# Order of work in the first four units of a fused linear attention and feed-forward kernel

## Chip, cores and metric

One core of one Trainium2 chip. The metric is the device time of one execution in microseconds (us), the median of the runs. The engines are called PE (matrix products), DVE (vector), ACT (scalar), POOL (GpSimd) and SP (the queue that issues nearly all transfers).

## What is computed

A gated linear attention is computed per batch and head, and its output goes through a feed-forward block with the "quick" GELU:

```python
# q, k, v, f_logit: (4, 8, 768, 48) float32
f = 1 / (1 + exp(-f_logit))
for t in range(768):
    state = f[:, :, t, :, None] * state + k[:, :, t, :, None] * v[:, :, t, None, :]
    y[:, :, t] = q[:, :, t] @ state
x = y.transpose(0, 2, 1, 3).reshape(3072, 384)
h = x @ w_in                      # w_in: (384, 2048), float64 in memory
g = h / (1 + exp(-1.702 * h))
out = g @ w_out                   # w_out: (2048, 384), float64 in memory
```

## The kernel before

**Units.** The 3072 tokens are cut into 12 units of 256 (three per batch), called `n` = 0 to 11 in the code and one to twelve in the titles of changes; here "unit one" is `n` = 0. `attention(n)` builds the pieces of one unit: for 64-token chunks the scores between tokens are built in six levels (distances 1, 2, 4 to 32). At each level PE multiplies queries by a copy of the keys (`score`, tile `sc`, line 416), DVE multiplies queries and keys by the decays of the next level (`promote`, L510 in the first units, L514 later), ACT copies the keys, and from unit four on the queries too, aside for the next level (`set_aside`, `Kc` L485 and `Qc` L491), and the scores are put through a mask into the matrix A (`evacuate`: level 0 by a multiplication on DVE, L457; the middle levels by predicated copies on DVE, L476; the last by four copies on ACT, L466). Then PE multiplies A by v into `y` (`add`, L525), PE forms each chunk's key-value sums (L634, into `pd` or the banks of `sc`), DVE rolls the states `st` forward (L655 to L659), PE adds the states' part to `y` (L680), ACT copies `y` to `yT` in eight pieces (L692), and transfers make `xT` of it (L723, L728), the input of the feed-forward block.

**Turning the inputs.** `turn` brings f, q and k into the layout with the head's channels on partitions: by PE transposes and ACT copies (L354, L359) for units one to three, by DVE transposes (L342) from unit four on. `half_up` (POOL, L369) finishes the decay's sigmoid, and `begin_gates` (POOL, L407) multiplies decays over growing distances into `tot`. `reverse_v` is DVE's shuffle of v (L306). `begin_f`, `begin`, `begin_k` and `begin_gates` start the next unit.

**Weights.** w_in and w_out arrive as 64-bit floats in 16 pieces. Each is converted by one ACT operation (L225, begun by `begin_pair`) and four DVE operations (L227 to L230). `convert` does one DVE operation at a time and asks for the next transfer after each piece. `merge(n, ..., pieces)` spreads `pieces` times two of these operations over unit `n`.

**Order.** PE's and POOL's order is the program's throughout. For units one to four (`opening`, then `merge` with `n` = 1, 2, 3) the order of all engines is written by hand up to `fill_order.close()`; after that a scheduler orders DVE, ACT and SP. `merge` walks the parts of a unit (`parts_of`) and puts feed-forward products of earlier units (`h` L1070, `o` L1084) between them as filling. In `parts_of` the last part of a unit, `inter` (the states' part of `y`, `yT` and `xT`), is run at the head of the next unit's first part, by `both`, for every `n` from 1 on. In unit three (`merge` with `n` = 2) the next unit, `n` = 3 = `N_FILL`, is begun by `begin_k`, which turns k, sets `Kc` and `Qc` aside and promotes.

**Banks.** The tile `sc` and the tile `y` have one buffer each of two PSUM banks; four further banks (`bank`) are handed round. `level(l)`, for units two and three, takes `sc` for every level:

```python
        def level(l):
            scores()
            score(0, l, queries(l))
            promote(l)
            evacuate(l)
            if l == 2:
                reverse_v(n)
```

Of the kernel before, what the change touches and what calls it, by code (L numbers as in the profile page):

```python
# [16 lines left out]
def view(t, offset, dims):  # L17

    a = t[:]
    return bass.AP(a.tensor, a.offset + offset, [list(a.ap[0])] + [list(d) for d in dims])  # L20
# [3 lines left out]
def kernel(  # L24
# [34 lines left out]
    B, H, S, D = q.shape  # L59
    DM = H * D  # L60
# [11 lines left out]
    NL = len(LEV)  # L72
# [4 lines left out]
    N_FILL = 3  # L77
# [49 lines left out]
    R = U // 32  # L127
# [64 lines left out]
    state = {"fetch": 0, "begin": 0, "done": 0, "behind": 0}  # L192
# [111 lines left out]
    def reverse_v(n):  # L304

        nc.vector.stream_shuffle(vts[n][:, 0], vrs[n], list(range(31, -1, -1)))  # L306
# [9 lines left out]
    def attention(n):  # L316
# [11 lines left out]
        parts = []  # L328
# [4 lines left out]
        def slot(s):  # L333
            return X[:, s]

        def turn(j, outs, fn=None, pieces=None):

            if n >= N_FILL:
                for f in (1, 0):
                    out = outs(f)  # L340
                    at, step = (0, 1) if f else (HALF - 1, -1)
                    nc.vector.transpose(  # L342
                        view(out, at, [[HALF, NP], [step, R4], [R4 * step, 32]]),
                        by_half[:, j, f].rearrange("p a (j d) -> p (a j) d", j=R4)[:, :, :32],
                    )
                if fn:
                    fn()
                return
            for j0 in pieces or range(0, R, 4):
                pt = bank([P, 4, P], f"t_{n}_{j}_{j0}")  # L350
                for jj in range(4):
                    for h in range(2):
                        x = (j0 + jj) * D
                        nc.tensor.matmul(  # L354
                            pt[h * HS:(h + 1) * HS, jj, :], lhsT=by_pair[j][:, h, x:x + HS], rhs=ident, start=True, stop=True
                        )
                for f in (1, 0):
                    at, step = (j0, 1) if f else (HALF - 1 - j0, -1)
                    nc.scalar.activation(  # L359
                        view(outs(f), at, [[HALF, NP], [R * step, 16], [step, 4]]),  # L360
                        pt.rearrange("p j (a f i) -> p f a i j", a=NP, f=2)[:, 1 - f],
                        (AF.Tanh if n else AF.Sigmoid) if fn else AF.Copy, scale=0.5 if fn and n else 1.0,
                    )
            if fn and n and (not pieces or R - 4 in pieces):
                half_up()


        def half_up():
            nc.gpsimd.tensor_scalar(F, F, 0.5, 0.5, op0=ALU.mult, op1=ALU.add)  # L369
# [18 lines left out]
            if n >= N_FILL or (n == 1 and 1 == 0):  # L388
                load_raw(n + 1, 1)

        def begin_k():
            turn(2, lambda f: slot((KR, KF)[f]))
            if n >= N_FILL or (n == 1 and 2 == 0):
                load_raw(n + 1, 2)
            if n >= N_FILL:
                set_aside(0, True)
                promote(0)
            else:
                set_aside(0)
# [35 lines left out]
        def scores(tag="sc"):  # L435
            new = ps.tile([P, 2, NP, 2, HS], F32, tag=tag, name=f"sc_{n}_{next(serial)}")
            t["sc"], t["both"] = (new[:, 0], new[:, 1]), [(0, new.rearrange("p h a s t -> p (h a) s t"))]
            return new
# [41 lines left out]
        def set_aside(l, q_too=False):  # L480


            m = LEV[l]
            c = t["Kc", l] = att.tile([P, SLOT], F32, tag="Kc", name=f"Kc_{n}_{l}", bufs=2)
            nc.scalar.copy(  # L485
                c.rearrange("p (n two m) -> p n two m", two=2, m=m),
                view(X, KF * SLOT, [[2 * m, SLOT // (2 * m)], [(KR - KF) * SLOT + m, 2], [1, m]]),
            )
            if q_too:
                c = t["Qc", l] = att.tile([P, 2, SLOT // 2], F32, tag="Qc", name=f"Qc_{n}_{l}", bufs=2)  # L490
                copied["aside"] = nc.scalar.copy(  # L491
                    c.rearrange("p f (n m) -> p f n m", m=m),
                    view(X, QR * SLOT, [[(QF - QR) * SLOT + m, 2], [2 * m, SLOT // (2 * m)], [1, m]]),
                )
# [35 lines left out]
                        )  # L530

        def level(l):
            scores()
            score(0, l, queries(l))
            promote(l)
            evacuate(l)
            if l == 2:
                reverse_v(n)
# [180 lines left out]
        def to_x(y, x, ng, hs=range(2)):  # L719

            for h in hs:
# [3 lines left out]
                while at < D:  # L725
# [4 lines left out]
                    )  # L730
                    at += w

        return (begin_f, begin, begin_k, begin_gates), parts, (open_level, open_evacuate, turn_k), lambda: reverse_v(n)

# [408 lines left out]


    units = [attention(n) for n in range(NALL)]
    LAG = 18 * DM

    def parts_of(n):  # L1150

        parts = list(units[n][1])
        _, inter = parts.pop()
        if n:
            kind, scores = parts[0]
            _, ahead = units[n - 1][1][-1]
            def both():
                rest = ahead()
                scores()
                if rest:  # L1160
                    rest()
            parts[0] = kind, both
        if n + 1 < NALL:
            begin_f, begin, begin_k, begin_gates = units[n + 1][0]
            i = len(parts)
            if n + 1 < N_FILL:

                parts.append(("K", lambda: (begin_k(), begin_gates())))
                kind, head = parts[0]
                parts[0] = kind, lambda: (head(), load_raw(n + 1, 1), keep_up(1))  # L1170
                parts.insert(4, ("B", lambda: (begin(), load_raw(n + 1, 2))))
                parts.insert(2, ("B", begin_f))
            else:
                kind, states = parts.pop()
                if n in CARRY:
                    parts += [("B", begin_f), ("B2", begin), ("S1", lambda: (states(), begin_gates())), ("K3", begin_k)]
                elif n < N_FILL:
                    second = parts[1][1]
                    parts[1] = parts[1][0], lambda: (second(), [load_raw(n + 1, j) for j in range(3)])
                    parts += [("B", begin), (kind, lambda: (states(), begin_gates())), ("B", begin_k)]  # L1180
                    parts.insert(i - 3, ("B", begin_f))
                else:
                    parts += [("B", begin_k), (kind, lambda: (states(), begin_gates()))]
                    parts.insert(i - 3, ("B", lambda: (begin_f(), begin())))
        else:
            parts.append(("W", inter))
        return parts
# [49 lines left out]
    UNIT = NFF * NK * U + U // P * NFF * DM  # L1237
    H20 = 20 * FG * G

    def opening():  # L1240

        begin_f, begin, begin_k, begin_gates = units[0][0]
        next_f, next_q, next_k, next_gates = units[1][0]
        level, evacuate, turn_k = units[0][2]
        load_raw(0, 0)
        load_raw(0, 2)
        load_raw(0, 1, (nc.scalar,))
        fetch_weights()
        begin_f()
        begin_gates()  # L1250
        begin_k()
        begin()
        load_raw(1, 0)
        load_raw(1, 2)
        load_v(0)
        load_raw(1, 1)
        fetch_weights()
        fetch_weights()
        for l in range(NL):
            chosen[:] = [2, 3][l % 2:][:1]  # L1260
            level(l)
            if l in (2, 3):
                next_f((0, 4)[l - 2:][:1])
            elif l < NL - 1:
                keep_up(1)
            if l == 1:
                begin_pair(0)
                state["begin"] = 1

        nc.scalar.activation(q_end, q_end, AF.Gelu_apprx_sigmoid)  # L1270
        chosen[:] = [2, 3]
        turn_k(0)
        turn_k(2)
        evacuate(0)
        evacuate(NL - 1)
        for l in range(1, NL - 1):
            evacuate(l)
            if l == 2:
                units[0][3]()
        chosen[:] = [2, 3, 2, 3]  # L1280
        next_q()
        units[0][1][-2][1]()
        next_gates()
        for _ in range(NOP):
            convert()

    fill = []
# [1 line left out]
    fill += mlp_blocks((0, 0)) + mlp_blocks((0, 1))  # L1289
    merge(1, fill, UNIT // 2 - LAG // 2 - 3 * DM, steady, 13, hold=1)  # L1290
    fill += mlp_blocks((1, 0), (1, 1)) + mlp_blocks((0, 2), (1, 2))
    merge(2, fill, UNIT + 3 * DM, steady, 10)
    fill += mlp_blocks((2, 0), (2, 1)) + mlp_blocks((2, 2), (0, 3)) + mlp_blocks((1, 3), (2, 3))
    w_sums = [*sums_of_w(("c3", "p15", "c2", "p6"))]
    merge(3, fill, 3 * UNIT // 2 - LAG // 2, steady, 7, by=0.7, chores=w_sums, per=1)
    fill_order.close()
    for n in range(N_FILL, NALL):
        fill += mlp_unit(n, fill)
# [42 lines left out]
```

## Time and profile before

| | |
|---|---|
| median of 3 runs | 611.32 us (608.47, 611.32, 612.24) |
| the profiled execution | 609.87 us, its span 608.0 us |
| mean granted clock of PE | 0.986 |
| PE busy | 579.3 us, 95% of the span |
| DVE, ACT, POOL busy | 436.0 (72%), 291.4 (48%), 139.2 (23%) us |
| transfers | 58.29 MB, mean 96 GB/s |

The span runs from the first to the last instruction. "Busy" counts an engine's instructions that compute; the granted clock is the share of full speed at which PE was let run. The page's 40 slices (15.2 us each; digits are busy tenths) show where PE is not full:

```profile
PE   7869899969999999999999999999999999999897
DVE  2797976565894867788867888868778686462284
PEclk9979999979999999999999999999999999999999
```

The opening and unit two fill the first five slices or so; unit three ends in the ninth (122 to 137 us). From 140 us on PE idles little. Instructions are listed with the line of the kernel, the engine, the operation and out<-in; an fp32 product of PE stands in the records twice.

### The profile page before, as it was taken

Reading aid. Unit: us, or ns where it says so; the run is one execution under the profiler, and the core shown is the slowest. Engines: PE = TensorE matmul, PEld = TensorE weight load, DVE = VectorE, ACT = ScalarE, POOL = GpSimd, SP = SyncE. Lnnn points to the kernel's source line nnn. Section 1 sums busy time; section 2 is a strip of 40 time slices with the busy share of each in tenths; the row PEclk is TensorE's granted clock in tenths of the full one; section 3 lists DMA queues with packets and bytes.
Section 4 is the critical chain, followed back from the end, with each engine's and each line's share of the span. In section 5 each row is a group of like instructions: output and inputs, shape, how many; then the busy total and the mean of one; then the engine's idle time right before and its main releaser. Section 6 shows DMA issues by size and latency. Waiting matters only on the chain.

```text
span 608.0 us, 18479 instructions
## 1 busy us (share of the span) xinstructions
PE 579.3 (95%) x7814; PEld 517.4 (85%) x7814; DVE 436.0 (72%) x696; ACT 291.4 (48%) x613; POOL 139.2 (23%) x215
## 2 busy tenths in 40 slices
PE   7869899969999999999999999999999999999897
PEld 6656676847677689999999999999999999999897
DVE  2797976565894867788867888868778686462284
ACT  4655643433332444456465474575474563552440
POOL 3030110050032523240421312502502502303000
PEclk9979999979999999999999999999999999999999
DMA  7856866652034245245443253443362111001000
GB/s 190 195 139 150 191 150 176 149 135 71 1 95 101 78 125 131 49 115 132 92 127 90 60 133 98 119 124 70 89 154 55 57 53 29 27 3 26 27 1 26
DMA packets 83314, 58.29 MB, mean 96 GB/s; under 512 B 33633, under 2 KB 75265, under 8 KB 83233
## 3 DMA queue, kind: packets, MB, share of 16 engines
q1 hardware_dynamic: 82896, 56.73, 37.5%
q8 instruction: 61, 1.00, 0.7%
q10 hardware_dynamic: 337, 0.39, 0.3%
q14 instruction: 20, 0.16, 0.1%
HBM read 43.98 MB, written 8.39 MB: 86 GB/s over the span
## 4 chain that ended last, share of the span: by engine, by line
PE 71%; DVE 12%; ACT 6%; DMA 4%; issue 3%; POOL 2%; SPq 2%; DVEq 0%; ACTq 0%; POOLq 0%
PE h L976 14%; PE h L1070 10%; PE o_Y L839 9%; PE o L1084 8%; PE o_Z L839 6%; PE sc L416 6%; PE h_y L976 5%; PE o_X L839 3%; PE o_W L839 3%; PE t L354 2%; ACT yT L692 2%; POOL tot L407 2%; PE y L680 1%; DVE g L1004 1%; DVE X L342 1%
## 5 line engine op out<-in xcount | busy, mean ns | idle before, releaser
L1070 PE MATMUL h<-xT,w_in 128*128 128x256 f32 x384 | 89.0, 387 | 1.6 <-DMA xT<-yT 1.6
L485 ACT COPY Kc<-X 128x512 f32<-128x512 f32 x72 | 48.2, 670 | 78.4 <-DVE X L514 57.4
L1070 PEld LDWEIGHTS h<-xT,w_in 128*128 128x128 f32 x384 | 73.1, 193 | 13.3 <-DMA xT<-yT 1.8
L514 DVE TENSOR_TENSOR X<-X,tot 128x1024 f32<-128x1024 f32 x45 | 57.4, 1275 | 35.7 <-PE sc L416 26.4
L1084 PE MATMUL o<-w_out,g 128*128 128x384 f32 x192 | 67.3, 500 | 3.7 <-DVE w_out L230 3.3
L1084 PEld LDWEIGHTS o<-w_out,g 128*128 128x128 f32 x192 | 36.1, 194 | 27.0 <-DVE w_out L230 4.1
L407 POOL TENSOR_TENSOR tot<-F 128x512 f32<-128x512 f32 x12 | 12.5, 1039 | 198.0 <-DVE st L658 192.3
L976 PE MATMUL h<-E,w_in 128*128 128x128 f32 (+1 forms) x420 | 53.4, 275 | 0.0
L839 PE MATMUL o_Y<-T,S 128*128 128x192 f32 x288 | 50.6, 329 | 0.0
L976 PEld LDWEIGHTS h<-E,w_in 128*128 128x128 f32 x420 | 50.1, 192 | 0.0
L1074 ACT ACTIVATE g<-h 128x256 f32<-128x256 f32 x64 | 24.0, 383 | 54.4 <-PE h L1070 54.1
L1006 ACT ACTIVATE g<-g 128x512 f32<-128x512 f32 (+1 forms) x63 | 35.5, 582 | 25.8 <-DVE g L1004 25.4
L839 PEld LDWEIGHTS o_Y<-T,S 128*128 128x128 f32 x288 | 46.8, 190 | 0.5
L692 ACT COPY yT<-y 48x256 f32<-48x256 f32 x96 | 35.1, 366 | 22.3 <-PE y L680 21.1
L476 DVE COPY_PREDICATED A<-masks,sc 128x256 f32<-128x256 uint32 (+1 forms) x98 | 42.1, 503 | 1.7 <-ACT A L466 1.6
L369 POOL TENSOR_SCALAR F<-F 128x1024 f32<-128x1024 f32 x11 | 16.1, 1461 | 111.5 <-ACT F L372 91.5
L1004 DVE TENSOR_TENSOR g<-g,h 128x512 f32<-128x512 f32 (+1 forms) x52 | 31.7, 631 | 12.5 <-PE h L976 11.5
L342 DVE STREAM_TRANSPOSE X<-raw 128x512 f32<-128x512 f32 x36 | 38.1, 1107 | 0.2
L416 PEld LDWEIGHTS sc<-X,Kc 48*64 48x64 f32 x1440 | 26.6, 138 | 12.1 <-ACT Kc L485 6.6
L416 PE MATMUL sc<-X,Kc 48*64 48x64 f32 x1440 | 31.2, 224 | 5.6 <-ACT Kc L485 2.7
L938 POOL TENSOR_TENSOR E<-xT 128x128 f32<-128x128 f32 (+1 forms) x32 | 17.7, 562 | 74.4 <-DMA xT<-yT 33.0
L1004 DVE TENSOR_TENSOR g<-g,h_y 128x512 f32<-128x512 f32 (+1 forms) x26 | 16.5, 633 | 22.0 <-PE h_y L976 21.1
(159 smaller groups left out, 1180.9 us busy)
## 6 DMA issues: line engine op xcount, KB each, us to landing
bits<-in_moe_w_out_dram SPq DMA_DIRECT2D x8, 768.0 KB
raw<-in_f_logit_dram SPq DMA_DIRECT2D x48, 96.0 KB
raw<-in_k_dram SPq DMA_DIRECT2D x48, 96.0 KB
bits<-in_moe_w_in_dram SPq DMA_DIRECT2D x8, 576.0 KB
raw<-in_q_dram SPq DMA_DIRECT2D x44, 96.0 KB
k_tok<-z SPq DMA_DIRECT2D x56, 64.0 KB
kt<-k_tok SPq DMA_DIRECT2D x14, 256.0 KB
xT<-yT SPq DMA_DIRECT2D x24, 144.0 KB
```

The source lines that it names most:

```text
L342: nc.vector.transpose(view(out, at, [[HALF, NP], [step, R4], [R4 * step, 32]]), by_half[:, j, f].rearrange("p a (j d) -> p (a j) d", j=R4) ...
L416: nc.tensor.matmul(t["sc"][h][g * HS:(g + 1) * HS, a, s, :], lhsT=t["Kc", l][rows(h), x:x + HS], rhs=rhs(h, a, g), start=True, stop=True,)
L476: moved = nc.vector.copy_predicated(out=view(A, c * HALF + at, dims), mask=mask.bitcast(U32), data=got)
L485: nc.scalar.copy(c.rearrange("p (n two m) -> p n two m", two=2, m=m), view(X, KF * SLOT, [[2 * m, SLOT // (2 * m)], [(KR - KF) * SLOT + m, ...
L514: nc.vector.tensor_tensor(x, x, y, ALU.mult)
L692: nc.scalar.copy(view(yT[rows(h)], at, [[U, NP], [step, HS]]), py[columns(h, g), g, :, f, :])
L839: nc.tensor.matmul(t[name], lhsT=lhs(f), rhs=rhs(f), start=(new and i == 0), stop=(i == HF - 1), skip_group_check=True,)
L976: nc.tensor.matmul(ph[:, t], lhsT=WA[a][:, f * P:(f + 1) * P], rhs=E[n][b], start=(root and t == 0), stop=not goes_on, skip_group_check=True,)
L1004: nc.vector.tensor_tensor(to, to, part, ALU.add if sign > 0 else ALU.subtract)
L1006: nc.scalar.activation(to, to, AF.Gelu_apprx_sigmoid)
L1070: nc.tensor.matmul(ph, lhsT=w_in[:, c, ff * P:(ff + 1) * P], rhs=xTs[n][:, c, :], start=(c == 0), stop=(c == NK - 1))
L1084: nc.tensor.matmul(t["po"], lhsT=g[ff // FG][:, ff % FG, tt * P:(tt + 1) * P], rhs=w_out[:, ff, :], start=(ff == ffs[0]), stop=(ff == ffs[ ...
```

## The change

```diff
@@ turn
-            if fn and n and (not pieces or R - 4 in pieces):
+            if fn and n and not pieces:
                 half_up()
@@ begin_k
-        def begin_k():
+        def begin_k(between=None):
...
                 set_aside(0, True)
+                if between:
+                    between()
                 promote(0)
@@ level
-            scores()
+            scores("y" if l in (2, 4) else "sc")
@@ parts_of
-        if n:
+        if n and n != N_FILL:
...
-                    parts += [("B", begin), (kind, lambda: (states(), begin_gates())), ("B", begin_k)]
+                    parts += [("B", begin), (kind, lambda: (states(), begin_gates())), ("B", lambda: begin_k(inter))]
@@ opening
-        evacuate(0)
-        evacuate(NL - 1)
-        for l in range(1, NL - 1):
+        for l in range(NL - 1):
             evacuate(l)
-            if l == 2:
+            if l == 0:
+                units[1][4]()
+            if l == 1:
                 units[0][3]()
         chosen[:] = [2, 3, 2, 3]
         next_q()
+        begin_pair(1)
+        state["begin"] = 2
+        evacuate(NL - 1)
         units[0][1][-2][1]()
@@ at the end
-    merge(2, fill, UNIT + 3 * DM, steady, 10)
+    merge(2, fill, UNIT + 3 * DM, steady, 12)
...
-    merge(3, fill, 3 * UNIT // 2 - LAG // 2, steady, 7, by=0.7, chores=w_sums, per=1)
+    merge(3, fill, 3 * UNIT // 2 - LAG // 2, steady, 5, by=0.7, chores=w_sums, per=1)
```

In the opening (unit one) the last level is put into A after the others instead of second, and it stands behind unit two's q turns and the ACT conversion of the second weight piece, which was begun later before. The shuffle of unit one's v (`units[0][3]`) comes after level 1 instead of level 2, and unit two's `half_up` (`units[1][4]`) after level 0 instead of with its f turns (`attention` returns it as a fifth item). In units two and three, levels 2 and 4 are formed in the banks of `y`. Unit three's `inter` moves from the head of unit four into `begin_k`, between the setting aside and the promotion of unit four's level 0. `pieces` goes from 10 to 12 in unit three and from 7 to 5 in unit four: four DVE operations, those of one weight piece, move forward.

## The prediction

> **What bounds the kernel now.** I read the page's 40 slices first, then busy time by stretches, then PE's waits, then the instructions in order of time around each stretch where PE is not full. In the stretches the columns are the stretch, its length, busy us (and instructions) of PE, weight loads, DVE, ACT and POOL, the granted clock, the DMA share and GB/s.
>
> ```profile
> 20.00:30.00 10.00, 7.45 (x158) 5.97 (x149) 7.89 (x19) 5.84 (x14) 1.50 (x1) 0.91 0.90 212
> 30.00:40.00 10.00, 6.55 (x206) 5.65 (x202) 9.59 (x16) 6.75 (x16) 4.73 (x6) 0.84 0.45 116
> 40.00:50.00 10.00, 8.38 (x93) 6.76 (x86) 6.98 (x13) 4.47 (x10) 0.88 (x1) 0.73 0.86 203
> ...
> 80.00:120.00 40.00, 40.00 (x401) 30.20 (x400) 24.70 (x43) 14.13 (x30) 1.04 (x1) 1.00 0.68 166
> 120.00:130.00 10.00, 5.58 (x18) 2.95 (x16) 8.11 (x12) 2.58 (x4) 7.78 (x9) 1.00 0.72 180
> 130.00:140.00 10.00, 8.78 (x140) 6.51 (x141) 5.72 (x8) 5.87 (x13) 0.08 (x1) 0.66 0.30 70
> 140.00:240.00 100.00, 99.62 (x1004) 77.19 (x1003) 72.54 (x99) 37.64 (x82) 24.79 (x21) 1.00 0.34 87
> ```
>
> PE is the bound: full from 80 to 120 and from 140 on. The change leaves PE's work as it is, so it can gain only PE's idle time before 140 us and the slow clock that goes with it. Three places hold them: the opening (20 to 46 us), unit two (46 to 80), and the end of unit three (120 to 137).
>
> DVE in the opening, then PE, DVE and ACT at the end of unit three (start, length, what; in brackets the idle time before it and who ended it):
>
> ```profile
> 22.87 0.74 DVE L457 TENSOR_TENSOR A<-sc,masks 128x256 f32<-128x256 f32 x2
> 25.26 1.98 DVE L476 COPY_PREDICATED A<-masks,sc 128x128 f32<-128x128 uint32 x6 [1.64 <-ACT A L466]
> ...
> 27.17 0.57 DVE L306 STREAM_SHUFFLE vt<-vr 128x384 f32<-128x384 f32 x1
> 27.64 1.41 DVE L476 COPY_PREDICATED A<-masks,sc 128x256 f32<-128x256 uint32 x4
> ```
>
> ```profile
> 125.02 3.49 PE L1084 MATMUL o<-w_out,g 128*128 128x384 f32 x10 [2.94 <-DVE w_out L230]
> 131.22 1.96 PE L680 MATMUL y<-X,st 48*48 48x64 f32 x64 [2.71 <-DVE X L514]
> ...
> 133.81 1.08 PE L416 MATMUL sc<-X,Kc 48*64 48x64 f32 x32
> ```
>
> ```profile
> 125.56 2.04 DVE L342 STREAM_TRANSPOSE X<-raw 128x512 f32<-128x512 f32 x2
> 129.18 1.98 DVE L514 TENSOR_TENSOR X<-X,F 128x1024 f32<-128x1024 f32 x1 [1.58 <-ACT Qc L491]
> ```
>
> ```profile
> 127.69 0.85 ACT L485 COPY Kc<-X 128x512 f32<-128x512 f32 x1 [5.68 <-DVE X L342]
> 128.45 0.65 ACT L491 COPY Qc<-X 128x512 f32<-128x512 f32 x1
> 131.20 0.69 ACT L485 COPY Kc<-X 128x512 f32<-128x512 f32 x1 [2.11 <-DVE X L514]
> 133.30 3.02 ACT L692 COPY yT<-y 48x256 f32<-48x256 f32 x8 [1.41 <-PE y L680]
> ```
>
> The reader is to see that ACT's copies of the last level (L466) hold DVE's other levels up for 1.64 us; and that PE stands twice, 2.94 us for a converted piece of w_out and 2.71 us for the promotion, while DVE and ACT work through a chain that ends in the Kc at 131.20.
>
> **Opening.** Nothing is added; evacuations, the shuffle and one ACT conversion (L225, 0.92) change places. DVE: 22.87 + 0.74 = 23.61, then 1.98 + 0.57 + 1.41 = 3.96 without the wait, so it ends at 27.57 instead of 29.05. PE's pd products wait for the shuffle, which now comes after level 1 (by about 25.5), so they follow the turns that end at 25.76: 25.8 + 0.31 + 0.33 + 1.38 = 27.8. The seven state operations (29.20 to 32.04, 2.84) then end at 30.6, 1.4 earlier. ACT: the four turns end at 26.85, the conversion at 27.77, the four copies of the last level (1.50) at 29.27. They stand ahead of the next turns on ACT and of y's products (L525) on PE; both come later. The conversion now stands ahead of these copies and needs its weights: they were issued at 17.90, and the latest that the trace allows for their landing is 27.77, when a transfer that waits for their place in the queue starts. In that worst case the copies end at 27.77 + 0.92 + 1.50 = 30.2, 0.9 later.
> PE's next turns took 3.21 at a low clock after an idle stretch (23.79's took 1.97 for the same 32). Without the idle time before them I have both ends: they end at 29.8 or 31.0. Then 0.1 + 0.66 + 0.85 + 0.12 (L359, Kc, the one-element copy) let PE's L680 start at 31.6 or 32.8, instead of 34.11: 1.3 to 2.5 earlier. Behind it come yT (3.02), its transfer (2.98 in the chain of waits) and the first h at 41.87, all with it. There the clock is half: h x12 took 4.56, and 2.79 where the clock is full. If the clock recovers at the same moment as now rather than sooner, the start is earlier at half speed and up to 2 x 2.79 - 4.56 = 1.0 is given back. So 0.3 to 2.5; I take 1.9, nearer to the upper end, because DVE's own chain (busy 9.59 of 10) is 1.4 earlier and PE's start more.
> The move of F's half_up alters nothing: POOL has no other work between 20.31 and 31.80, and its order is the same. The shuffle's move lets v's next transfers start about 2 us earlier (27.77 now) on SP; nothing waits behind them before 35.28.
>
> **Two levels in y's banks.** PE waits once for sc's bank (1.0 us on DVE's A at 59.99). But DVE is busy 9.69, 9.44 and 9.65 of 10 from 50 to 80, and PE's next wait, 0.84 for DVE's X before the transposes at 63.02, grows by what this one loses. Gain 0, bounds 0 and 1.0; the new owner of the banks, y, has been copied out by 38.4 and 76.6, before levels 2 need them.
>
> **Conversions.** Four operations move from unit four to unit three: 0.58 + 0.55 + 1.04 + 1.0 = 3.2 us of DVE (means of L227 to L230), plus one ACT piece of 0.92 and a weight transfer ahead of the next raw loads on SP. Cover: DVE's 15.3 idle us of 80 to 120, and 3.74 more before the states at 119.37. If that cover were gone, 3.2 us would fall on the states. The raw k that is needed at 125.56 is issued ahead of the added transfers, by 96.8. The w_out that PE waits for is then ready: the 2.94 wait goes. What is late next follows.
>
> **y ahead of the promotion.** ACT and PE keep their order, so Kc and Qc, then yT (eight copies), then the second Kc now stand in this order on ACT; and the promotion now waits for y's products on PE. I walk it at today's times (the shift of the opening applies to all). PE: o from 120.63, 10 records, 1.45 + 6 x 0.335 (5.36 for 16) = to 124.1; y (0.98 for 64 at full clock, from 1.96 at half) to 125.1, its states being ready at 122.06; two more o (4 records, 1.34) to 126.4. Then scores, which need Qc. DVE: states to 122.06, conversions 1.70 + 1.25 + 0.57 as now to 125.6, a sum that the new order puts ahead (0.55), transposes 2.04: 128.2 instead of 127.6. ACT: Kc and Qc to 129.7. So PE idles 126.4 to 129.7, has 0.7 of scores, and then needs the second Kc: promotion 129.7 to 131.7 at the slow 1.98, but yT holds ACT from 129.7 to 132.7, Kc to 133.4. The second scores start at 133.4 to 133.5, and stand at 133.81 now, with the same products done by then. The two waits of 5.65 become 3.3 and 3.0. Gain 0.3; bounds: +1.8 (below) and -2.0, if DVE's pieces run at the speeds they have without POOL beside them (1.04 and 1.02 for 1.70 and 1.25, and 1.23 for the promotion).
> The clock's row: 0.66 in 130 to 140, after these waits; o x18 took 7.39, at full clock 18 x 0.335 = 6.0; y and the scores lose 1.0 and 0.8. That cost of about 3.2 stays, since a longer idle stretch remains.
> The Trainium skill, "TensorE: Matmul & The Clock Gate", section "HAM oscillation — how this bites in real kernels", speaks against the change: a gap of about one 3.4 us window halves the clock, and a full busy window is needed to restore it. By that rule 3.4 to 6.8 us run at half speed after 133.4, a cost estimated at 1.7 to 3.4, and my sum would be 1.5 better to 0.2 worse.
>
> **Sum.** 1.9 + 0 + 0 + 0.3 = 2.2 us. The profiled execution took 609.87 (span 608.0 and 1.87 around it), which gives 607.7; the median of the runs shown is 1.45 above it, so 609.1, called 609. Own range of this case: gains of 0 to 5, 606.3 to 611.3, and a little for the scatter (608.47 to 612.24 shown).
>
> **Rivals.** (A) Both waits of unit three really close, and the clock stays up: 2.94 + 2.71 + about 3.2 on top of 1.9, 10.8 us, so 600.5; only the idle time, 7.5, so 603.8. For it: both named causes are removed. Against: the scores still need Kc and Qc, which hang on DVE's transposes. (B) Slower: yT on ACT in front of the second Kc becomes the bound. From today's 131.89 (Kc done) it costs 3.02 + 0.55: the scores at 135.5 instead of 133.81, plus 1.7 of a longer slow clock (half of the 3.4 us by which the idle stretch grows), some 3.5, with the opening's gain given back to the clock: 614.8. It decides once DVE's transposes end later than about 128.6. For it: they are at 128.2 in my walk. Against: Kc's and yT's rows all shift with the earlier states.
>
> **Numbers.** Forecast 0.64, A 0.23, B 0.13. Range 603 to 613: it leaves out half of A and half of B, and a little of the forecast. About 1% (6.1 us) is what a measurement can tell from no change: below 605.2 lies nearly all of A and a sliver of the forecast, 0.24; above 617.4 the tail of B, 0.05; within, 0.71.
>
> **What would show it.** The 1.64 wait on L466's writer gone, y's L680 of unit one near 32; no wait on w_out near 120; instead a wait of the scores for Qc and another for the second Kc, with yT between them on ACT; the clock again below 0.8 in 130 to 140. Wrong if PE starts o after these scores more than 4 us earlier than 134.81 (A), or later (B).

## The result and the profile after

| | before | after |
|---|---|---|
| median | 609.65 us (20 runs, 607.69 to 613.03) | 609.55 us (20 runs, 608.66 to 610.97) |
| profiled execution, span | 609.87, 608.0 | 609.56, 607.6 |
| mean granted clock | 0.986 | 0.986 |

The ratio is 0.9999, with a 95% interval of 0.9986 to 1.0012: no difference, and at most 0.9 us gained or 0.7 lost. The forecast of 609.0 lies near the measured 609.55, but by luck: it was added up as 609.87 - 2.2 + 1.45, the last being the distance from the profiled execution to a median of three runs (611.32), and over 20 runs the median before is 609.65. Of the 2.2 us of gain nothing is seen; they lie outside the interval. Busy time by stretches of the changed kernel, columns as before:

```profile
20.00:30.00 10.00, 8.84 (x218) 7.46 (x216) 9.49 (x23) 7.61 (x18) 1.50 (x1) 1.00 1.02 234
30.00:40.00 10.00, 4.77 (x182) 3.58 (x178) 9.72 (x15) 6.05 (x16) 4.74 (x6) 0.96 0.46 117
...
120.00:130.00 10.00, 6.97 (x84) 4.27 (x82) 8.12 (x13) 2.62 (x5) 7.36 (x9) 1.00 0.68 174
130.00:140.00 10.00, 7.06 (x75) 4.57 (x76) 5.80 (x7) 5.87 (x13) 0.52 (x1) 0.66 0.36 86
140.00:240.00 100.00, 100.00 (x1007) 77.62 (x1006) 67.58 (x95) 36.62 (x81) 23.85 (x21) 1.00 0.31 79
```

In the opening PE does more from 20 to 30 (8.84 for 7.45) and stands longer from 30 to 40 (4.77 for 6.55, of which a part was slow: the clock was 0.84 there and is 0.96): what came earlier waits later. From 120 to 140 PE was busy 14.36 us and is busy 14.03, with the same low clock, 0.66, behind the gaps. From 140 on it has become full (100.00 for 99.62).

PE of the changed kernel in order of time, the opening and then the end of unit three (start, length, what; in brackets the idle time before and who ended it; lines of this kernel are 2 higher than before):

```profile
30.08 0.31 PE L527 MATMUL y<-A,vt 64*48 64x64 f32 x2
31.21 1.10 PE L527 MATMUL y<-A,vt 64*48 64x64 f32 x62 [0.82 <-issue]
32.58 1.04 PE L682 MATMUL y<-X,st 48*48 48x64 f32 x46 [0.27 <-ACT y L647]
...
34.78 0.46 PE L418 MATMUL sc<-X,Kc 48*64 48x64 f32 x14 [0.81 <-issue]
...
42.05 4.82 PE L1072 MATMUL h<-xT,w_in 128*128 128x256 f32 x12 [3.73 <-DMA xT<-yT]
...
124.37 1.11 PE L682 MATMUL y<-X,st 48*48 48x64 f32 x64
125.41 1.56 PE L1086 MATMUL o<-w_out,g 128*128 128x384 f32 x4
130.01 0.69 PE L418 MATMUL sc<-Qc,Kc 48*64 48x64 f32 x32 [3.04 <-ACT Qc L493]
133.64 1.13 PE L418 MATMUL sc<-X,Kc 48*64 48x64 f32 x32 [2.93 <-ACT Kc L487]
134.70 7.80 PE L1086 MATMUL o<-w_out,g 128*128 128x384 f32 x18
```

ACT of the same kernel in the second of these places:

```profile
129.31 0.65 ACT L493 COPY Qc<-X 128x512 f32<-128x512 f32 x1
129.86 3.03 ACT L694 COPY yT<-y 48x256 f32<-48x256 f32 x8
132.91 0.67 ACT L487 COPY Kc<-X 128x512 f32<-128x512 f32 x1
```

The old waits of 2.94 (w_out) and 2.71 (promotion) are gone, and 3.04 (Qc) and 2.93 (the second Kc, behind yT) stand in their place, but with only 0.69 us of products between them, where there were 3.49. In the opening y is earlier (32.58, was 34.11), but it and the scores behind it stall 0.8 us each on "issue" (no releaser that the profile names), and h waits 3.73 us for xT, where it waited 1.62. This execution was also 1.41 us late before any edit could act: the first transposes of unit one's promoted keys (`tkn`, L586 before, L588 here) start at 23.90, and at 22.49 in the profile before. Times in the opening are therefore best counted from these transposes, as is done below.

### The profile page after: what moved, and what is told of

It reads as the page before. It is cut to its first block, busy times and chain, and to the rows that moved or that the text cites. A ratio compares the mean times of both kernels' runs of the same rounds, so it can differ in the third digit from the quotient of the medians.

```text
span 607.6 us, 18475 instructions
## 1 busy us (share of the span) xinstructions
PE 578.6 (95%) x7814; PEld 516.3 (85%) x7814; DVE 432.2 (71%) x696; ACT 291.5 (48%) x613; POOL 139.9 (23%) x215
## 4 chain that ended last, share of the span: by engine, by line
PE 74%; DVE 13%; ACT 5%; issue 3%; DMA 2%; POOL 2%; SPq 1%; DVEq 0%; ACTq 0%; POOLq 0%
PE h L978 15%; PE h L1072 12%; PE o L1086 9%; PE o_Y L841 9%; PE o_Z L841 6%; PE h_y L978 5%; PE sc L418 5%; PE o_X L841 3%; PE o_W L841 3%; ACT yT L694 2%; POOL tot L409 2%; PE t L354 1%; DVE X L512 1%; DVE st L660 1%; DVE st L661 1%
## 5 line engine op out<-in xcount | busy, mean ns | idle before, releaser
L369 POOL TENSOR_SCALAR F<-F 128x1024 f32<-128x1024 f32 x11 | 17.4, 1582 | 114.0 <-ACT F L372 91.6
```

## Experiments

Theory 1: the opening's earlier y is taken back by xT, whose transfers stand behind a w_out piece in SP's queue. Theory 2: at the end of unit three PE stands because no other product lies where the chain of Kc, Qc, yT and Kc holds the scores. Theory 3 came after the first four runs: joining the two gaps lets the half clock fall on the scores and o in every execution, and not only in some. "Unit three's y" is the product of A and v in that unit (L525 at 117.27 us before, L527 at 117.69 after); the recorded expectations call it the second y. Each ratio below is to the kernel before, run on the same chip beside it; "the changed kernel" stands at 0.9999 in its own comparison.

**The opening alone, e1** (the kernel before with the opening's hunks of the change).

> The kernel before with the opening's edits alone (order of the evacuations, shuffle, F's half-sum, Kc and Qc of unit one earlier). Theory 1 (the earlier y is taken back by xT, whose transfers wait in SP's queue behind the transfer of a piece of w_out): y's products of unit one start 1.4 to 2.9 us earlier than 34.11, the first h stays within 0.6 us of 41.87 with a wait for xT of 3 us or more, and the whole is 0 to 0.6 us shorter. The prediction's own sum (nothing takes it back): the first h 1.9 us earlier and the whole 1.9 shorter, ratio 0.997.

Ratio 0.9979 (0.9967 to 0.9991): 1.3 us faster, more than theory 1 allowed and less than the prediction's 1.9. y starts at 32.03, h at 41.23 after a wait of 3.23 for xT. So the opening pays, and something else in the change costs about as much. Its profile shows one more thing: at the end of unit three the clock stayed at 1.00, although nothing there was altered.

```profile
130.00:140.00 10.00, 9.35 (x152) 6.39 (x152) 6.56 (x10) 6.53 (x14) 0.00 (x0) 1.00 0.28 60
```

**xT ahead of the weights, e2.**

```diff
@@ fetch_weights
+        if state.get("later"):
+            state["later"] += 1
+            return
@@ both (after inter)
+                if state.get("later"):
+                    owed, state["later"] = state["later"] - 1, 0
+                    for _ in range(owed):
+                        fetch_weights()
@@ opening
         next_gates()
+        state["later"] = 1
```

> The changed kernel, with the weight transfers that the opening's last conversions ask for issued behind xT's of unit one instead of ahead of them. Theory 1: xT lands 1 to 2.5 us earlier after yT, the wait of the first h for xT falls from 3.7 us to 1 to 2.5, and the whole is 1 to 2 us shorter than the changed kernel (ratio 0.997). Rival (the opening is held by VectorE, busy over 9.4 of 10 us to 80, or by the low clock of 39 to 46 us): h may start earlier, but the whole is the same within 0.4 us; the piece of w_out then lands later and could cost some of it again.

Ratio 0.9983 (0.9970 to 0.9996), 1.0 us below the kernel before; against the changed kernel the intervals overlap. PE of this kernel:

```profile
41.32 4.62 PE L1075 MATMUL h<-xT,w_in 128*128 128x256 f32 x12 [2.04 <-DMA xT<-yT]
```

The wait for xT is 2.04, and from yT's end to the first h there are 3.94 us, where the changed kernel has 5.21. The same stretch is 3.24 to 5.01 in four profiles of the old opening (mean 4.15), 4.73 to 5.63 and, once, 3.68 in seven of the new one (mean 4.89), and 3.71 to 4.20 in the three with xT first (mean 3.95). So the piece ahead of xT takes some 0.7 us back, half of what theory 1 said, and putting xT first returns it; in the whole time that is not told apart from the scatter, and this run's y was itself held 1.53 us on "issue". From the first transposes of the promoted keys to the first h the same profiles take 19.2 us on average with the old opening, 18.2 with the new one and 17.3 with xT first: 1.0 us of the lead reaches h, and 1.9 with xT first.

**yT ahead of Kc and Qc, e3.**

```diff
@@ begin_k
-                set_aside(0, True)
                 if between:
                     between()
+                set_aside(0, True)
                 promote(0)
```

> The changed kernel, with y, yT and xT of unit three put ahead of the Kc and Qc copies as well, not only ahead of the promotion and the second Kc. Theory 2 (the order on ScalarE holds the second scores): yT runs at 125.5 to 128.5 in ScalarE's idle time, the second Kc follows the promotion at once, the second scores start at 131.5 to 132.6 instead of 133.64, the whole is 1 to 2 us shorter. Rival (VectorE's transposes and the promotion hold them; yT's place is covered): the second scores within 0.4 us of 133.64, no change.

Ratio 0.9978 (0.9967 to 0.9988), about 1.3 us faster than the changed kernel. yT ran at 124.19 to 127.22 in ACT's idle time, the wait for the second Kc fell from 2.93 to 1.56. From unit three's y to the second scores it takes 14.67 us and took 15.95: 1.28 less. So yT's place on ACT costs what theory 2 says. The clock is still halved here, and at the h behind o 0.87 of the 1.28 is left in this profile (the table below).

**Filling moved behind y, e4.** The last part of unit three gets five shares of the filling, not one.

```diff
-                    parts += [..., ("B", lambda: begin_k(inter))]
+                    parts += [..., ("B3", lambda: begin_k(inter))]
@@ merge: converting
-{..., "T": 1, "B": 1}
+{..., "T": 1, "B": 1, "B3": 1}
@@ steady
-        return {..., "B": 1, "K": 1}.get(kind, 0)
+        return {..., "B": 1, "B3": 5, "K": 1}.get(kind, 0)
```

> The changed kernel, with the last part of unit three given five shares of the filling products instead of one, so that some 6 us of h and o products come between y and the scores, which are taken from the stretch of 80 to 120 us. Theory 2 (TensorE stands at the scores for lack of other work that could go there): the two waits of 3.0 and 2.9 us shrink to under 1.5 together, the clock stays at 1.0 through 130 to 140, the whole is 5 to 9 us shorter (ratio 0.985 to 0.992). Rival (the stretch of 80 to 120 is then bound by VectorE's states, so the idle time only moves ahead to 110 to 120): TensorE idles there for as long as it gains, the whole changes by under 2 us.

Ratio 0.9904 (0.9879 to 0.9929): 5.9 us faster. The stretches of this kernel, and PE ahead of them:

```profile
120.00:130.00 10.00, 10.00 (x128) 7.03 (x126) 8.12 (x8) 5.06 (x13) 7.46 (x9) 1.00 0.87 204
130.00:140.00 10.00, 9.54 (x72) 6.48 (x65) 7.28 (x10) 4.04 (x9) 0.00 (x0) 1.00 0.15 35
```

```profile
112.23 2.86 PE L1072 MATMUL h<-xT,w_in 128*128 128x256 f32 x12 [1.90 <-DVE sum L1138]
```

PE is full but for 0.46 us and the clock is 1.00. Of the two waits 0.46 is left; a new one of 1.90, of h for DVE's sums, appears from 110 on, in the stretch that gave the products away, so the rival is right for a part. Theory 2 stands.

**The rest alone, f1** (the changed kernel with the opening of before).

> The changed kernel with the opening put back as it was before: what is left is levels 2 and 4 in y's banks, the moved conversions and the earlier y. Theory 3 (TensorE's idle time at the end of unit three, 2.94 and 2.71 us with 6.2 us of work from start to start between them, becomes 3.0 and 2.9 us with 0.7 between them, so the clock is halved there in every execution and not only in some): 0.7 to 1.5 us slower than before (ratio 1.001 to 1.0025), the profile with the half clock. The prediction's own sum: 0.3 us faster.

Ratio 1.0034 (1.0021 to 1.0048): 2.1 us slower than before. The sign of what the prediction adds up for these edits (0 + 0 + 0.3 us of gain) is wrong, and theory 3's direction is right; the measured loss is 0.6 above its upper end of 1.5, which lies within the interval.

**Idle products in the two gaps, f3** (7 and 6 of them). The second set overwrites the scores of one level of unit four, so that level is left out of the result; the other work is as it was.

```diff
@@ levels
-            scores()
+            new = scores()
+            fill_up(7)
             score(0, l, queries_aside(l))
+            fill_up(6)
             score(1, l + 1, queries(l + 1))
```

> The changed kernel with 7 and 6 products of the identity with the masks (128x320, 0.4 us each, into the bank that the scores then overwrite) ahead of the first and the second scores of unit four, in TensorE's two gaps of 3.0 and 2.9 us; nothing else of the order is altered. Theory 3: the gaps stay, the clock is 1.0 in 130 to 140, o x18 takes 6.0 to 6.1 instead of 7.80, the whole is 2 to 2.5 us shorter than the changed kernel (ratio to before 0.996). Rival (the half clock costs little, since VectorE and ScalarE are late next): within 0.6 us of the changed kernel.

Ratio 0.9980 (0.9968 to 0.9993). PE of this kernel:

```profile
126.01 3.93 PE L550 MATMUL sc<-masks,ident 128*128 128x320 f32 x14
129.88 0.69 PE L418 MATMUL sc<-Qc,Kc 48*64 48x64 f32 x32
130.50 3.50 PE L550 MATMUL sc<-masks,ident 128*128 128x320 f32 x12
133.93 0.70 PE L418 MATMUL sc<-X,Kc 48*64 48x64 f32 x32
134.56 6.07 PE L1094 MATMUL o<-w_out,g 128*128 128x384 f32 x18
```

The clock stays at 1.00: o x18 takes 6.07 for 7.80, the scores 0.70 for 1.13. But a product took 0.56 us, not 0.4, so the second scores came 17.03 us after unit three's y, 1.08 later than in the changed kernel. Still the h behind o starts 1.08 earlier (23.57 us after that y, 24.65 there). The half clock therefore costs the changed kernel 1.08 + 1.08 = 2.2 us from the second scores to h; the idle products themselves give half of it back, so the whole gained about 1.2 us, not the 2 to 2.5 expected.

**Conversions back to 10 and 7 (e7); y back behind the promotion (e5).** Two runs, each the changed kernel with that hunk undone.

> The changed kernel with the conversions put back to 10 in unit three and 7 in unit four; y stays ahead of the promotion. Theory 3: the wait of o for w_out (about 2.9 us) is back and covers the wait for Qc, one wait for Kc of about 2.9 remains, with several us of products between the two, so the clock falls in only a part of the executions: 0.3 to 1.2 us faster than the changed kernel. The prediction's walk, which gives the moved conversions no gain and no loss: the same within 0.3 us.

> The changed kernel with y, yT and xT of unit three put back behind the promotion. The prediction's walk: 0.3 us slower than the changed kernel. Theory 3: one idle stretch of over 5 us before y, half clock in every execution, the same as the changed kernel within 0.5 us. Rival B of the prediction (yT on ScalarE in front of the second Kc costs): 1 us faster or more.

The first: 1.0011 (0.9996 to 1.0027), not faster than the changed kernel. Theory 3's number for it falls: I had taken the wait for w_out to return in full, and it is 1.54 us, since y and four o now run ahead of it; 0.62 for Qc and 2.93 for Kc follow, and the clock is halved from 132.21. The second: 1.0007 (0.9995 to 1.0019), one wait of 5.93 us before y, half clock from 131.77. It is not told apart from the changed kernel; a gain of 1 us (rival B) isn't there. So with either edit undone PE's idle time still lies together ahead of the second scores (0.62 and 2.93 with 0.69 of products between, or 5.93 in one piece), and the half clock falls there in both profiles. The rise of 0.3 us that the prediction's walk gives for y put back is too small to be seen.

**The kernel before, profiled twice more (b1, b2).**

> The kernel before once more, for its clock. Theory 3 in its sharper form (the clock is judged in windows of 3.41 us that run on by themselves; in the kernel before, a half clock that the first gap, 2.94 us before o, sets off runs out while TensorE would wait for the promotion anyway, and only one that the second gap sets off slows the scores and o x18): the time from the second y (L525) to the h behind o x18 is 24.8 us only if the half clock begins at the scores; it is 21.9 to 23.0 if it begins at o x10 or not at all. The two waits are 2.9 and 2.7, or the second less where o x10 is slow. The time from the end of the opening's half clock to the second y is 71.2 to 72.2. Rival (the difference of the medians comes from the transfers or the start): 24.8 again whatever the clock.

> The same as the run ahead of it, at another place of the clock's windows: 24.8 us from the second y to the h behind o x18 if the half clock begins at the scores, 21.9 to 23.0 otherwise; in the changed kernel and its variants it was 23.8 to 24.8 in every profile in which the filling was not moved.

608.84 and 609.47 us. PE of the first:

```profile
125.94 4.94 PE L1084 MATMUL o<-w_out,g 128*128 128x384 f32 x10 [2.94 <-DVE w_out L230]
132.14 1.11 PE L680 MATMUL y<-X,st 48*48 48x64 f32 x64 [1.27 <-DVE X L514]
...
134.12 6.07 PE L1084 MATMUL o<-w_out,g 128*128 128x384 f32 x18
140.03 1.46 PE L1070 MATMUL h<-xT,w_in 128*128 128x256 f32 x6
142.13 5.05 PE L1070 MATMUL h<-xT,w_in 128*128 128x256 f32 x22 [0.64 <-DVE sum L1136]
```

The half clock came with o x10 (4.94 us, 3.49 at full clock) and ate into the wait for the promotion (1.27, was 2.71); behind it all runs at full speed. The second profile is the same (5.00, 1.20). From unit three's y to the h behind o x18 they take 21.85 and 21.84 us, as theory 3 said (21.9 to 23.0); from the end of the opening's half clock to that y it is 71.2 and 71.1, where 71.2 to 72.2 was expected. The profile that the prediction was made from takes 24.77. By stage, in us, every kernel whose filling was not moved:

| order at the end of unit three | unit three's y to h | h to the end of the span | sum |
|---|---|---|---|
| before: the profile predicted from | 24.77 | 465.96 | 490.7 |
| before: b1, b2, and e1 (opening alone) | 21.85, 21.84, 21.85 | 466.87, 466.83, 466.81 | 488.7 each |
| changed: after, e2, f1 | 24.65, 24.54, 24.84 | 465.26, 465.29, 465.21 | 489.9, 489.8, 490.1 |
| y back (e5), conversions back (e7) | 24.79, 24.42 | 465.26, 466.19 | 490.1, 490.6 |
| yT first (e3), idle products (f3) | 23.78, 23.57 | 465.24, 465.33 | 489.0, 488.9 |

In three of four profiles with the order of before, the half clock cost nothing there (e1 had none, b1 and b2 spent it ahead of a wait); in all six with the order of after, with one of its two edits or with yT first it fell on the scores and o.

**Three edits together (e8)**, those of e2, e3 and e4 on the changed kernel, and the same with four shares of filling (e9).

> The changed kernel with three edits together: the weight transfers of the opening behind xT's, yT of unit three ahead of Kc and Qc, and five shares of the filling between y and the scores. Theory 2: the second scores follow the first with a wait under 0.3 us, clock 1.0 in 130 to 140, 6.5 to 7.5 us shorter than before (ratio 0.988 to 0.989). Rival (the filling moved by five shares already covers the chain, yT's place no longer matters and the opening's transfer gives nothing): 5.9 shorter as with the filling alone.

> The same three edits with four shares of the filling instead of five. With yT ahead of Kc and Qc the chain to the second scores is about 1 us shorter, so four shares leave a wait for Qc of under 1 us and h's wait of 1.9 us for the sums at 110 becomes shorter: 6 to 8 us shorter than before. Rival (every product that stays ahead of y is missing in the gap): 1 us or more slower than with five shares.

0.9883 (0.9863 to 0.9903) and 0.9861 (0.9843 to 0.9879), medians 601.72 and 601.03: 7.1 and 8.5 us faster than before, both faster than before and after. With five shares both waits are gone; with four, a wait of 0.91 for the second Kc remains, and h no longer waits for the sums at 110. The two intervals overlap, so which number of shares is better stays open. PE of the second:

```profile
125.85 0.69 PE L421 MATMUL sc<-Qc,Kc 48*64 48x64 f32 x32
127.46 0.70 PE L421 MATMUL sc<-X,Kc 48*64 48x64 f32 x32 [0.91 <-ACT Kc L490]
128.09 6.07 PE L1089 MATMUL o<-w_out,g 128*128 128x384 f32 x18
```

## Why the prediction was right in its number and wrong in three of its terms

**Opening, 1.9: mis-sized; 1.3 (0.5 to 2.0) by the run that has it alone.** Counted in the profiles, from the first transposes of the promoted keys to unit three's y, it is 1.4 (95.1 us on average in four of the old opening, 93.7 in six of the new one), and 2.1 with xT first (93.0, one profile). What was to show it did: the wait on L466 is gone, and y starts at 32.58. Three things made it smaller. First, the row it was valued from was one execution's. The turns' 3.21 us at half clock, which the sum took as removed, are there in two profiles of the old opening (3.21, 3.35) and not in the two others (1.97 in b2 and in the rest alone): where the clock was up anyway, only the prediction's lower end of 1.3 is to be had. Second, behind yT the transfer of xT takes longer, as said for the run with xT first; the prediction let "its transfer (2.98 in the chain of waits)" follow y unaltered and did not ask what stands ahead of it in SP's queue. Third, probably, PE's instructions: the records of the instruction queue show pieces of 16 KB, and where PE stands on "issue" it goes on 1.2 to 1.65 us after one has landed. Read from the records of four executions:

```
kernel   piece landed  y goes on   next piece landed  scores go on
after    29.80         31.21       33.43              34.78
e1       29.05         30.54       32.64              33.84
e2       30.37         31.80       33.93              35.37
e9       29.65         30.93       33.26              34.51
```

In b1 the pieces land at 29.49 and 33.20 too, and PE, which gets there later, doesn't stand for them. This is read and fits every profile of the new opening; no run took the fetch away, so its cost (0.8 + 0.8 us in the changed kernel, 1.5 for y alone in e2) isn't tested.

**y's banks, 0: right.** From unit two's level 2 to unit three's y it takes 69.01 us before, 68.99 after, 69.02 with the rest alone.

**Conversions, 0: wrong in size, a gain of 0.7 or more by the profiles.** The cover named for them held; nothing was lost in 80 to 120 (PE is busy for all 40.00 us). But the four operations are missing after 140, where the prediction had looked for no gain: from h to the end it takes 465.2 to 465.3 us with them moved and 466.0 to 466.9 without, in part DVE's sums, for which h waits 0.64 in b1. The run that undoes this edit alone has 466.19 for 465.26; in its whole time, 0.7 us, that is not clear of the scatter.

**y ahead of the promotion, +0.3: the walk was right, its base was not.** It put the end of o at 126.4, Qc at 129.7 and the second scores at 133.4; with the 0.42 us by which this profile is later at unit three's y, the trace has 126.97, 129.96 and 133.64. The waits were to be 3.3 and 3.0 and are 3.04 and 2.93. The step that failed is "The clock's row: [...] That cost of about 3.2 stays, since a longer idle stretch remains." It stays in the changed kernel, though at 2.2 us and not 3.2 (the row of 3.2 counts 1.0 for y, which the walk itself already runs at full clock); the estimate of 1.7 to 3.4 that the prediction sets beside it covers the 2.2. But the kernel before pays it in some executions only: in one of the four profiles of its order, the one predicted from. There, 3.49 us of o lie between the gaps, and a half clock set off by the first is spent while PE would wait anyway. Against those executions the order of after loses 24.65 - 21.85 = 2.8 us by the h behind o and gets back 466.8 - 465.3 = 1.5 later: 1.3 us net, the lower end of what the rest alone measured (2.1; 1.3 to 2.9). Averaged over all four profiles of the old order, the slow one among them, the sum by stage is 489.2, and 489.9 in the three of the changed order: 0.7 of loss, so a part of the 2.1 stays unexplained. The rest alone and the opening alone add up to 0.8 us of loss, where 0.1 of gain was measured for both; intervals of 0.7 to 0.8 to each side allow that.

**Rivals.** A (both waits close, 600.5 to 603.8) was refuted for this change, and its prices were near: the run that closes all but 0.46 us of them alone (e4) is at 603.6, though it waits 1.90 elsewhere, and those with yT and xT moved too are at 601.0 and 601.7. B (slower by yT on ACT) was refuted in its size, but the run with yT first shows that yT's place costs 1.3 us.

## What to carry to other kernels

A wait that is removed is worth something only if the next operation in the same queue can run: here the two waits of 5.65 us came back as 5.97, until products were put between y and the scores, which gave 5.9 us (and 7.1 or 8.5 together with yT moved ahead and xT first). Two idle stretches that are joined can cost more than the same two apart, because a clock that falls after the first is no longer paid for in the second. And one profile is one place of the clock's windows: before a slow row is counted as removable, see whether a second profile has it.

## What was not expected of the hardware

**The clock's windows and where they lie.** All stretches of half clock in the 14 profiles, but for the one that the end of each execution cuts off, last 3.41 us or a multiple, at places that differ from execution to execution. The Trainium skill, "TensorE: Matmul & The Clock Gate", section "Part 1: The HAM clock gate", gives 3413 ns for a window that runs on freely, and the traces agree. Its section "HAM oscillation — how this bites in real kernels" puts the danger at idle gaps over about 3.4 us; here gaps of 2.94 (b1, b2) and 2.71 us (before) were enough. Cut into these windows, those at the end of unit three in which PE was busy for a share of 0.36 or less were followed by half clock (0.36 before, 0.27 in b1, 0.24 in b2, 0.20 or less in the changed kernel, e2, e3, e5 and f1). Those with 0.42 (e5), 0.48 (before) and 0.44 and 0.55 (e1) were not, and one with 0.48, partly of narrow score products (e7), was. The share alone is not the whole rule: in the opening, with its many narrow products, windows of 0.59 were followed by half clock in the kernel before and in b1, and one of 0.59 in f1 was not.

**The start scatters by 2.5 us.** The first transposes of unit one's promoted keys (L586 of before), ahead of which no kernel was altered, start between 22.23 and 24.75 us. Of the three profiles with a half-clock window at 15 to 19 us, all are in the upper part (23.90, 24.32, 24.75).

**Instructions can be late.** The Trainium skill, "Runtime: NRT & Kernel Launch", section "Instruction fetch mechanics", says that instructions are fetched in blocks of 16 KiB, ahead of their use and mostly unseen. The block size is that of the traces; unseen they seem not to be where PE passes many narrow products in a row: up to 2.2 us of "issue" (f3) stand ahead of y's products in the new openings. That these stalls are the fetch is read from the landings above and was not tested.
